# Weight-block sums of six pairs made early and kept in DRAM, and the transposes' PSUM tile cut in two, in a local-attention and feed-forward kernel

## The chip, the cores and the metric

The kernel runs on one NeuronCore of a Trainium2 chip. The metric is the device time of one execution in microseconds. Three runs of the kernel before took 658.18, 658.39 and 658.76 us (median 658.39). Engines are called PE (TensorE matmuls), PEld (TensorE weight loads), DVE (VectorE), ACT (ScalarE), POOL (GpSimd) and SP (SyncE, which only issues DMAs here).

## The reference

Attention over a window of 96 keys and 8 global keys, then a two-layer feed-forward block:

```python
scores = q @ k.T / 8 + bias            # batch 4, heads 8, sequence 768, head_dim 64
a = softmax(scores where global or 0 <= rel < 96)
x = (a @ v)  ->  [3072, 512]
h = x @ w_in                           # [512, 2048]
g = maximum(0.01 * h, h)
out = g @ w_out                        # [2048, 512]
```

All of it is float32. A product of two fp32 matrices is made of three matmuls with operands split into a high and a low part (high*high, high*low, low*high).

## The kernel before

**Work.** The 3072 tokens are 24 steps of 128 tokens, and a step is two units of four heads: 48 units. A unit u runs through loads (Lk, Lv, Lq), scores on PE (S, line 316), bias and row minimum on DVE (B, line 333), exponentials on ACT (E, line 349), sums on DVE (N), the turn of the probabilities, the product with v on PE (V, line 470) and a copy to the feed-forward's input (Xh, lines 480 and 489; Xl). Units 0 to 15 turn the probabilities on PE (T, line 421, against diagonal matrices that POOL makes, G, line 398) into a PSUM tile `ps_tr`, whose two halves are copied to SBUF by two steps, K (half 0, ACT, line 437) and k (half 1; on DVE, line 435, for units 0 to 5, else on ACT). Units from 16 on divide (M, line 386), transpose on DVE (D, line 391) and pass through DRAM (`via`: the store belongs to D, the four fetches are I).

**Feed-forward, chunks 0 to 2.** The steps are cut in chunks of 3, 3, 2, 4, 4, 4, 4. For the first three chunks and each of the 16 column blocks f of w_in there is F (the products with w_in, lines 1030 to 1032), four gate steps g (a ACT line 1042, b DVE line 1044, c ACT line 1046, d DVE line 1048) and H (the products with w_out, lines 1066 to 1068). Meanwhile the weights come in as 32 pieces (Lw) and are turned from float64 words to high and low parts by conversions c (a ACT, b three DVE instructions at lines 801, 803 and 807, c ACT line 811, d DVE line 814).

**Feed-forward, chunks 3 to 6.** Each has 512 tokens and works by pairs p of column blocks, eight pairs to a chunk, 32 in all (Q, y, d, r, h, l, J with the pair's number 0 to 31). The first layer of a pair is a 2x2 block product done with seven block products instead of eight (Q, line 698), which needs four sums of weight blocks. The copy y (ACT, line 729) and line 735 (d, DVE) join the products, line 739 (r) is the leaky maximum, line 742 (h) the high part on ACT, line 745 (l) the low part on DVE, and J (line 753) the product with w_out. Outputs leave by U (lines 759 on DVE, 761 on ACT).

**The sums.** `combine` (lines 652 to 685) makes the four sums of a pair in 16 steps C: 12 on POOL (line 662) and 4 on ACT (line 665, the rounding to a high part). Before the change the sum h1 goes back in place over the w_in block it came from, and the other three go into the place of w_out blocks 4 to 15 in SBUF. So w_out is first stored to DRAM (O, line 706, 16 stores of 512 KB), and only four of its blocks are in SBUF at a time from then on, reloaded through POOL's DMA queue for every pair (R, line 709). The sums are made once, in the first of the four chunks, and stay for the other three.

**Order.** `ORDER` (line 39) is a string of words, one per step, written out beforehand. `step` and `late` issue each word's instructions, and `pin` keeps them in that order on their engine. All engines, and the DMA queues of SP and POOL, take their instructions in this order and none passes another. In the kernel before, the first C stands between F39 and H38, and pair p's sums run beside the products of pair p-2 or p-1 up to pair 6.

Of the kernel before, what the change touches and what calls it, by code (L numbers as in the profile page):

```python
# [67 lines left out]
V20 g34a N22 H33 Xh20 g34b Lv23 M22.0 g34c M22.1 F35 g34d M22.2 M22.3 H34 D22 g35a g35b S23 g35c I22 F36 B23.0 g35d
E23.0 B23.1 H35 B23.2 E23.1 Lk26 B23.3 g36a Lq13 E23.2 g36b V21 E23.3 g36c N23 F37 Lv24 Xh21 g36d M23.0 M23.1 H36
M23.2 g37a M23.3 g37b F38 D23 g37c g37d S24 g38a H37 g38b I23 B24.0 g38c B24.1 E24.0 F39 B24.2 C0.0 E24.1 g38d Lk27  # L70
E24.2 B24.3 C0.1 E24.3 H38 g39a C0.2 N24 g39b C0.4 V22 C0.3 M24.0 g39c M24.1 C0.5 S25 g39d Lv25 Xh22 F40 M24.2 C0.6
Lk28 B25.0 B25.1 Lq14 E25.0 A3.1 B25.2 E25.1 B25.3 H39 g40a M24.3 E25.2 D24 E25.3 C0.8 g40b F41 Y3.4 C0.11 N25 C0.7
I24 g40c M25.0 C0.10 C0.9 V23 M25.1 g40d g41a C0.12 S26 g41b Xh23 Lv26 C0.14 M25.2 H40 C0.13 M25.3 Lk29 g41c B26.0
A3.2 g41d E26.0 F42 B26.1 B26.2 E26.1 A3.3 B26.3 E26.2 D25 H41 E26.3 z3.4 g42a A3.4 Y3.5 F43 Y3.1 g42b I25 N26 C0.15
g42c Y3.6 M26.0 V24 z3.1p g42d g43a S27 M26.1 Lv27 Xh24 g43b H42 Lk30 z3.6p M26.2 g43c M26.3 Lq15 g43d F44 D26 C1.0
# [1068 lines left out]
```

## Time and profile before

| | |
|---|---|
| runs, us | 658.18, 658.39, 658.76 |
| the profiled execution's own time, us | 657.92 |
| its span, us | 656.0 |
| PE busy, us (share of span) | 623.5 (95%) |
| DVE busy, us | 497.8 (76%) |
| ACT busy, us | 280.3 (43%) |
| POOL busy, us | 191.5 (29%) |
| granted TensorE clock over the span | 0.992 of full |
| DMA moved | 118.05 MB, 180 GB/s |

Busy PE means that some matmul was in flight; a gap shorter than a matmul's latency does not show as idle. The span is the recorded program; the own time is what the run's clock says for the same execution, 1.9 us more.

### The profile page before, as it was taken

The page shows a single profiled execution, that of the slowest core. Times are in us where ns is not written, and L with a number is a line of the kernel's source. Part 1 is how long each engine was busy: PE and PEld are TensorE (multiplying, and loading weights), DVE is VectorE, ACT ScalarE, POOL GpSimd, SP SyncE. Part 2 cuts the span into 40 slices and gives each one's busy share as a digit, 9 for nine tenths or more (in the row PEclk, how much of TensorE's full clock was granted, in tenths as well). Part 3 has the DMA queues.
Part 4 walks back from the last instruction along what each step waited for, and adds up shares of the span by engine and source line. Part 5 has one row for each costly group of instructions (what it writes and reads, how often), then busy time and mean ns, then how long its engine had stood idle before and what let it go on. Part 6 is the DMA issues. An engine that isn't in the chain of part 4 may idle for free. (4 is left out here: it accounts for less than half of the span.)

```text
span 656.0 us, 16093 instructions
## 1 busy us (share of the span) xinstructions
PE 623.5 (95%) x6188; PEld 535.1 (82%) x6188; DVE 497.8 (76%) x1277; ACT 280.3 (43%) x801; POOL 191.5 (29%) x265
## 2 busy tenths in 40 slices
PE   5679999999999999989999999999999999999995
PEld 4568888998888877778788888888888888889894
DVE  7899998965766689898997977778977747654542
ACT  4878766546444464523344342334442314211111
POOL 3332410003200067978774200014200015100100
PEclk9799999999999999999999999999999999999999
DMA  8756644497665444527667586775686543433331
GB/s 291 264 197 202 210 160 145 151 409 263 186 195 180 153 152 123 161 92 201 184 196 192 165 279 190 211 213 181 200 269 179 164 121 98 157 101 97 97 97 69
DMA packets 61604, 118.05 MB, mean 180 GB/s; under 512 B 8784, under 2 KB 27216, under 8 KB 61520
## 3 DMA queue, kind: packets, MB, share of 16 engines
q1 hardware_dynamic: 52880, 85.48, 40.6%
q0 software_dynamic: 8640, 31.46, 16.1%
q8 instruction: 51, 0.84, 0.5%
q14 instruction: 33, 0.27, 0.2%
HBM read 90.18 MB, written 26.74 MB: 178 GB/s over the span
## 5 line engine op out<-in xcount | busy, mean ns | idle before, releaser
L742 ACT CAST rounded<-room 128x512 fp32r<-128x512 f32 x64 | 39.7, 620 | 193.5 <-DVE room L739 186.0
L709 POOL DMA_DIRECT2D wo<-w x60 | 32.7, 545 | 229.1 <-PE ps_two L753 221.1
L753 PE MATMUL ps_o<-wo,rounded 128*128 128x512 f32 x320 | 95.1, 394 | 0.5 <-DVE rounded L745 0.5
L753 PE MATMUL ps_two<-wo,rounded 128*128 128x512 f32 x320 | 95.2, 395 | 0.0
L349 ACT ACTIVATE pr<-pr,nmall 128x192 f32<-128x192 f32 (+1 forms) x192 | 83.7, 439 | 14.6 <-DVE nmall L333 14.4
L735 DVE TENSOR_TENSOR room<-ps_o,room 128x256 f32<-128x256 f32 x128 | 53.9, 421 | 34.5 <-PE ps_o L698 26.9
L735 DVE TENSOR_TENSOR room<-ps_q,room 128x256 f32<-128x256 f32 x96 | 40.3, 420 | 32.4 <-PE ps_q L698 30.9
L1030 PE MATMUL ps_h<-rounded,wih 128*128 128x384 f32 (+1 forms) x192 | 62.7, 326 | 1.9 <-ACT atz L1042 1.9
L1031 PE MATMUL ps_h<-rounded,wih 128*128 128x384 f32 (+1 forms) x192 | 61.0, 318 | 0.1
L1032 PE MATMUL ps_h<-rounded,wil 128*128 128x384 f32 (+1 forms) x192 | 61.0, 318 | 0.0
L739 DVE SCALAR_TENSOR_TENSOR room<-room 128x512 f32<-128x512 f32 x64 | 59.4, 927 | 1.9
L753 PEld LDWEIGHTS ps_o<-wo,rounded 128*128 128x128 f32 x320 | 53.7, 188 | 6.7 <-DVE rounded L745 1.0
L753 PEld LDWEIGHTS ps_two<-wo,rounded 128*128 128x128 f32 x320 | 54.0, 188 | 6.1
L698 PEld LDWEIGHTS ps_o<-rounded,wo 128*128 128x128 f32 x384 | 53.9, 188 | 6.2 <-DVE room L735 0.7
L698 PE MATMUL ps_o<-rounded,wo 128*128 128x256 f32 x384 | 56.2, 282 | 0.0
L333 DVE CUSTOM_DVE_ANT_0 pr<-ps_av,nbw 128x192 f32<-128x192 f32 x140 | 42.2, 352 | 13.6 <-ACT room L480 8.1
L698 PE MATMUL ps_q<-rounded,wih 128*128 128x256 f32 x256 | 48.3, 282 | 2.9 <-ACT room L729 2.9
L698 PEld LDWEIGHTS ps_q<-rounded,wih 128*128 128x128 f32 x256 | 41.3, 188 | 6.9 <-ACT room L729 3.9
L386 DVE TENSOR_SCALAR pr<-pr,rs 128x192 f32<-128x192 f32 (+1 forms) x128 | 43.6, 383 | 0.7
L1044 DVE SCALAR_TENSOR_TENSOR atz<-atz 128x384 f32<-128x384 f32 (+1 forms) x48 | 27.2, 567 | 20.7 <-ACT atz L1042 20.6
L1030 PEld LDWEIGHTS ps_h<-rounded,wih 128*128 128x128 f32 x192 | 36.1, 188 | 6.7 <-ACT atz L1042 2.7
L470 PEld LDWEIGHTS ps_av<-room,vr 64*64 64x64 f32 x1472 | 30.5, 134 | 13.2 <-PE ps_two L753 7.1
(134 smaller groups left out, 1433.8 us busy)
## 6 DMA issues: line engine op xcount, KB each, us to landing
wo<-w POOLq DMA_DIRECT2D x60, 512.0 KB, 4.0
via<-pr SPq DMA_DIRECT2D x28, 384.0 KB, 2.7
room<-via SPq DMA_DIRECT2D x112, 96.0 KB, 3.8
kr<-in_kp_dram SPq DMA_DIRECT2D x40, 256.0 KB, 4.0
vr<-in_vp_dram SPq DMA_DIRECT2D x40, 256.0 KB, 3.8
room<-in_wo_dram SPq DMA_DIRECT2D x16, 512.0 KB, 4.4
room<-in_wi_dram SPq DMA_DIRECT2D x16, 512.0 KB, 4.5
w<-wo SPq DMA_DIRECT2D x16, 512.0 KB, 7.6
```

The source lines that it names most:

```text
L333: pin(nc.vector.tensor_tensor_reduce(out=head(u, pr, a, j), in0=own(u, ps[:, j, a * KW:(a + 1) * KW]), in1=nb, scale=-0.125, scalar=3.0e38 ...
L349: pin(nc.scalar.activation(out=p, in_=p, func=AF.Exp, scale=-1.0, bias=nm[:, 2 * a + j:2 * a + j + 1], accum_out=sm[:, 2 * a + j:2 * a + j ...
L386: pin(nc.vector.tensor_scalar(out=p, in0=p, scalar1=rs[:, n:n + 1], scalar2=1.0, op0=ALU.mult, op1=ALU.mult))
L698: tc.keep_in_program_order(nc.tensor.matmul(out, lhsT=lhs[:, k], rhs=rhs[:, k], start=k == 0 and m == 0, stop=k == 1 and m == 2))
L709: pin(nc.gpsimd.dma_start(out=woboth[:, f % 4], in_=w2[f]))
L735: pin(nc.vector.tensor_tensor(out=quarter[i][o], in0=lps[b][:, h * HB:(h + 1) * HB], in1=quarter[a][q], op=ALU.add))
L739: pin(nc.vector.scalar_tensor_tensor(out=t, in0=t, scalar=0.01, in1=t, op0=ALU.mult, op1=ALU.max))
L742: pin(nc.scalar.copy(out=lg(i)[0], in_=lt[i]))
L753: tc.keep_in_program_order(nc.tensor.matmul(o, lhsT=lhs, rhs=rhs, start=f == 0 and m == 0, stop=f == NF - 1 and m == 2))
L1030: tc.keep_in_program_order(nc.tensor.matmul(ps, lhsT=wih[:, k, fs], rhs=xh[:, k, :CT], start=(k == 0), stop=False))
L1031: tc.keep_in_program_order(nc.tensor.matmul(ps, lhsT=wih[:, k, fs], rhs=xl[:, k, :CT], start=False, stop=False))
L1032: tc.keep_in_program_order(nc.tensor.matmul(ps, lhsT=wil[:, k, fs], rhs=xh[:, k, :CT], start=False, stop=(k == NK - 1)))
```

## The change

Pairs 0 to 5 (`NVIA = 6`) get their sums in a work area of SBUF of 8 KB per partition (`early_sums`), not in place. A step b stores the finished area of a pair to a new DRAM tensor `cw` (1 MB, SP's queue). Two steps e load it back through POOL's queue: e.0 brings the three sums h2, h3, h4 (768 KB) to the same region of w_out's place that `combined` reads, e.1 the sum h1 (256 KB) over its w_in block. Pairs 6 and 7 make their sums in place as before. In the new order the first C stands between the last weight conversions, ahead of F19, and the sums of pair 5 end at F41; those of pairs 6 and 7 run beside the products of pairs 0 and 1. The conversions stand up to three pieces earlier (25 pieces end ahead of F17 before, 28 now). w_in's high and low parts become one tile, with a block's halves side by side, so that a sum's operands are 256 elements in a row. And the PSUM tile of two banks that T, the accumulators of chunk 2 and two of J's accumulators use becomes two tiles of one bank each.

```diff
+NVIA = 6
+EARLY_AT = (8, 0, 8, 8, 8, 8)
...
-M23.2 g37a M23.3 g37b F38 D23 g37c g37d S24 g38a H37 g38b I23 B24.0 g38c B24.1 E24.0 F39 B24.2 C0.0 E24.1 g38d Lk27
...
+O2 g17d c31a F18 c30b O3 O4 H17 c31b c30c g18a O5 g18b c31c C0.0 O6 F19 c30d g18c C0.1 g18d O7 c31d C0.2 H18 g19a O8
...
-        ps = ps_x.tile([P, 2, 512], F32, tag="ps_t", name="ps_tr")
+        ps = [ps_x.tile([P, 512], F32, tag=f"ps_t{f}", name="ps_tr") for f in range(2)]
...
-        src = d["ps"][:, :, :6 * HALF].rearrange("p f (j g q) -> p f j g q", j=2, g=3)[:, f, :, g0:]
+        src = d["ps"][f][:, :6 * HALF].rearrange("p (j g q) -> p j g q", j=2, g=3)[:, :, g0:]
...
-                two = ps_x.tile([P, 2, DM], F32, tag="ps_t", name="ps_two")
-                acc[c] = [two[:, tt] for tt in range(CHUNKS[c])]
+                acc[c] = [ps_x.tile([P, DM], F32, tag=f"ps_t{tt}", name="ps_two") for tt in range(CHUNKS[c])]
...
+    cw = dram.tile([NVIA, P, 4, 2, 2 * P], F32, name="cw", bufs=1)
+
+    def early_sums(p):
+        return at(EARLY_AT[p], [8, 2 * P])
...
-        (h2, l2), (h3, l3), (h4, l4) = (combined(p, m) for m in range(3))
-        t1, t2, t3 = (at(o, [2, P]) for o in (14, 15, 20))
-        eng = nc.gpsimd
+        if p < NVIA:
+            b = [early_sums(p)[:, x].rearrange("p (a b) -> p a b", a=2) for x in range(8)]
+            t2, t1, t3 = b[1::2][:3]
+            (h2, l2), (h3, l3), (h4, l4), (h1, l1) = ([x.bitcast(F32R) for x in b[2 * m:2 * m + 2]] for m in range(4))
+        else:
+            t1, t2, t3 = (at(o, [2, P]) for o in (14, 15, 20))
+            (h2, l2), (h3, l3), (h4, l4) = (combined(p, m) for m in range(3))
+            h1, l1 = h21, l21
...
+        elif what == "b":
+            pin(nc.sync.dma_start(out=cw[n].rearrange("p m x d -> p (m x) d"), in_=early_sums(n)))
+        elif what == "e":
+            if part == ".0":
+                to, m = sums3[:, n].rearrange("p m x a b -> p (m x a b)"), slice(0, 3)
+            else:
+                to, m = wiboth[:, 2 * n + 1, 0].rearrange("p x d -> p (x d)"), slice(3, 4)
+            pin(nc.gpsimd.dma_start(out=to, in_=cw[n, :, m].rearrange("p m x d -> p (m x) d")))
```

Three places of the order follow. Line numbers are those of the kernel before and, in the second fence of each, of the changed kernel (line 662 becomes 675, 709 becomes 722, 435 becomes 438, 759 becomes 780).

The first is POOL from the second reload for pair 4 (`wo<-w` is a reload R) to the first for pair 5; the additions between are sums of pair 6. Before:

```order
L709 DMA wo<-w_152 128x1024
L662 TENSOR_TENSOR room<-wih,wil 128x256
L662 TENSOR_TENSOR room<-room 128x256
L662 TENSOR_TENSOR room<-wih,wil 128x256
L662 TENSOR_TENSOR room<-room 128x256
L662 TENSOR_TENSOR wil<-room,wih 128x2x128
L662 TENSOR_TENSOR room<-room 128x256
L662 TENSOR_TENSOR room<-wih,wil 128x256
L662 TENSOR_TENSOR wo<-room,wo 128x256
L709 DMA wo<-w_152 128x1024
```

and now, from the first reload for pair 2 (the three additions are the last of pair 7's sums) to the second for pair 7:

```order
L722 DMA wo<-w_151 128x1024
L675 TENSOR_TENSOR wo<-room,wo 128x256 x3
L722 DMA wo<-w_151 128x1024 x9
L736 TENSOR_TENSOR room<-room 128x512
L722 DMA wo<-w_151 128x1024 x2
```

Of the sums nothing is left here: after pair 7's last, which now come as early as pair 2's reloads, POOL has reloads alone up to the differences of the next chunk's inputs (line 736, 715 before).

The second is DVE in the front of the program, around step k of an early unit. Before:

```order
L807 SCALAR_TENSOR_TENSOR awz<-room,awz 128x512 [waits DVE_49]
L374 TENSOR_SCALAR rs<-sm 128x4 [waits Activation_49,Pool_49]
L375 RECIPROCAL rs<-rs 128x4 [waits DVE_49]
L435 COPY room<-ps_tr 128x2x3x64 [waits Activation_49]
L333 ISA pr,nmall<-ps_sc,nbw 128x192
```

and now:

```order
L828 SCALAR_TENSOR_TENSOR awz<-room,awz 128x512 [waits DVE_49]
L377 TENSOR_SCALAR rs<-sm 128x4 [waits Activation_49,Pool_49]
L378 RECIPROCAL rs<-rs 128x4 [waits DVE_49]
L438 COPY room<-ps_tr 128x2x3x64 [waits PE_49]
L336 ISA pr,nmall<-ps_sc,nbw 128x192
```

The copy k waits for PE's transposes alone, no longer for ACT's copy K.

The third is DVE at the end of the program, the last two output copies U. Before:

```order
L739 SCALAR_TENSOR_TENSOR room<-room 128x512 [waits DVE_49]
L770 TENSOR_LOAD flag [waits DVE_49]
L745 TENSOR_TENSOR btz<-room,rounded 128x512 [waits PE_49,Activation_49]
L759 COPY room<-ps_o 128x512 [waits PE_49,Pool_49]
L759 COPY room<-ps_two 128x512 [waits Activation_49]
```

and now:

```order
L760 SCALAR_TENSOR_TENSOR room<-room 128x512 [waits DVE_49]
L791 TENSOR_LOAD flag [waits DVE_49]
L766 TENSOR_TENSOR btz<-room,rounded 128x512 [waits PE_49,Activation_49]
L780 COPY room<-ps_o 128x512 [waits PE_49,Pool_49]
L780 COPY room<-ps_two 128x512 [waits PE_49]
```

The last copy, too, waits for PE where it waited for ACT's copy of the other bank.

## Rows read from the trace of the kernel before

**Rows 1.** The page's head and its part 1, PE.

```profile
span 656.0 us, 16093 instructions
...
PE 623.5 (95%) x6188; PEld 535.1 (82%) x6188; DVE 497.8 (76%) x1277; ACT 280.3 (43%) x801; POOL 191.5 (29%) x265
```

**Rows 2.** Busy time by stretch: stretch, length, busy us (x instructions) per engine, clock, DMA.

```profile
10.00:48.00 38.00, 27.58 (x653) 23.13 (x650) 33.98 (x114) 28.32 (x91) 14.27 (x24) 0.91 0.73 256
48.00:130.00 82.00, 82.00 (x910) 70.94 (x909) 74.89 (x179) 56.66 (x148) 17.58 (x30) 1.00 0.55 173
130.00:205.00 75.00, 75.00 (x723) 64.19 (x721) 50.95 (x150) 37.93 (x110) 9.74 (x16) 1.00 0.75 259
205.00:241.00 36.00, 36.00 (x452) 30.43 (x451) 24.57 (x81) 17.83 (x62) 7.85 (x10) 1.00 0.49 154
241.00:263.20 22.20, 20.13 (x143) 16.01 (x142) 21.51 (x46) 11.58 (x38) 16.92 (x19) 1.00 0.41 125
263.20:286.60 23.40, 21.58 (x203) 17.84 (x201) 21.11 (x47) 11.48 (x35) 22.30 (x28) 1.00 0.44 136
286.60:354.10 67.50, 63.33 (x610) 52.97 (x610) 60.47 (x125) 22.40 (x68) 44.17 (x58) 1.00 0.63 181
354.10:414.30 60.20, 60.20 (x590) 52.29 (x586) 47.98 (x135) 23.83 (x70) 14.25 (x16) 1.00 0.69 210
```

**Rows 3.** Waits: who for whom, us in total, times, longest.

```profile
ACT wo L665 <- POOL room L662: 13.5, 10, 2.5
...
PE ps_q L698 <- ACT room L729: 2.9, 4, 1.0
...
DVE room L435 <- ACT room L437: 2.1, 2, 1.2
```

**Rows 4.** Timeline from 27 us, ACT and DVE: start, length, instruction, [idle before].

```profile
27.10 0.48 ACT L437 COPY room<-ps_tr 128x384 f32<-128x384 f32 x1 [0.80 <-PE ps_tr L421]
...
27.61 0.56 DVE L435 COPY room<-ps_tr 128x384 f32<-128x384 f32 x1 [0.92 <-ACT room L437]
```

**Rows 5.** Groups by form, POOL, whole span: busy us, mean ns | idle before.

```profile
L709 POOL DMA_DIRECT2D wo<-w x60 | 32.7, 545 | 229.1 <-PE ps_two L753 221.1 <-PE ps_fl L766 3.7 <-DVE rounded L745 3.7
L662 POOL TENSOR_TENSOR room<-room 128x256 f32<-128x256 f32 x32 | 27.8, 872 | 1.8
...
L662 POOL TENSOR_TENSOR wo<-room,wo 128x256 fp32r<-128x256 f32 x24 | 17.9, 755 | 3.0 <-ACT wo L665 2.9
```

**Rows 6.** Groups by form, DVE, 263.2 to 354.1 us.

```profile
L739 DVE SCALAR_TENSOR_TENSOR room<-room 128x512 f32<-128x512 f32 x14 | 20.1, 1435 | 0.4
L735 DVE TENSOR_TENSOR room<-ps_o,room 128x256 f32<-128x256 f32 x28 | 11.6, 416 | 1.1 <-PE ps_o L698 0.5
L386 DVE TENSOR_SCALAR pr<-pr,rs 128x192 f32<-128x192 f32 x24 | 10.7, 484 | 0.1
...
L745 DVE TENSOR_TENSOR rounded<-room,rounded 128x512 fp32r<-128x512 f32 x7 | 8.7, 1244 | 0.0
```

**Rows 7.** Groups by form, DVE, 378.3 to 402.5 us.

```profile
L735 DVE TENSOR_TENSOR room<-ps_o,room 128x256 f32<-128x256 f32 x8 | 3.4, 425 | 1.8 <-ACT pr L349 1.0 <-PE ps_o L698 0.6
L739 DVE SCALAR_TENSOR_TENSOR room<-room 128x512 f32<-128x512 f32 x4 | 2.8, 692 | 0.1
...
L745 DVE TENSOR_TENSOR rounded<-room,rounded 128x512 fp32r<-128x512 f32 x2 | 1.4, 682 | 0.0
```

**Rows 8.** Groups by form, DVE, 130 to 205 us.

```profile
L386 DVE TENSOR_SCALAR pr<-pr,rs 128x192 f32<-128x192 f32 x24 | 6.3, 317 | 0.2
...
L803 DVE SCALAR_TENSOR_TENSOR awz<-room,awz 128x512 int32<-128x512 int32 x5 | 3.5, 692 | 0.2
```

**Rows 9.** Line 706, the sixteen stores O of 512 KB: issue to landing.

```profile
DMA to landing us min/median/max: 3.8/7.6/7.8
```

**Rows 10.** Timeline from 646 us, ACT and DVE, the last two copies.

```profile
648.73 0.59 ACT L761 COPY room<-ps_two 128x512 f32<-128x512 f32 x1 [1.56 <-PEq L1086]
649.35 0.69 DVE L759 COPY room<-ps_two 128x512 f32<-128x512 f32 x1 [1.31 <-ACT room L761]
```

More of the change, by code (lines that the diff above doesn't have):

```diff
@@ L161, in fast_path @@
 @with_exitstack
[L162 removed]
+def fast_path(ctx, tc, qp, kp, vp, wi, wo, nvec, weights, wiboth, woboth, nmall, out, B, H, S):
     nc = tc.nc
@@ L642, in fast_path @@
     quarter = [[x[:, h * HB:(h + 1) * HB] for h in range(2)] for x in lt]
+    sums3 = woboth.rearrange("p f x d -> p (f x d)")[:, 8 * DM:].rearrange("p (q m x a b) -> p q m x a b", q=NF // 2, m=3, x=2,
+                                                                   a=2)
     def combined(p, n):
-        i, half = divmod(3 * p + n, 2)
-        return [w[:, 4 + i, half * 2 * P:(half + 1) * 2 * P].rearrange("p (a b) -> p a b", a=2) for w in (woh, wol)]
+        return [sums3[:, p, n, x] for x in range(2)]
+    cw = dram.tile([NVIA, P, 4, 2, 2 * P], F32, name="cw", bufs=1)
+    def early_sums(p):
+        return at(EARLY_AT[p], [8, 2 * P])
     def first_weights(p, row, col):
-        fs = slice((2 * p + row) * P, (2 * p + row + 1) * P)
-        return [w[:, 2 * col:2 * col + 2, fs] for w in (wih, wil)]
+        return [w[:, 2 * p + row, col].rearrange("p (a b) -> p a b", a=2) for w in (wih, wil)]
     def combine(p, n):
@@ L1025, in products @@
     wih, wil = weights[:2]
[L1026 to L1027 removed]
+    NK = wih.shape[2] * wih.shape[3] // P
     ps = psum.tile([P, CT], F32, tag="ps_h", name="ps_h")
     for k in range(NK):
[L1030 to L1032 removed]
+        wh, wl = (w[:, f, k // 2, k % 2 * P:(k % 2 + 1) * P] for w in (wih, wil))
+        tc.keep_in_program_order(nc.tensor.matmul(ps, lhsT=wh, rhs=xh[:, k, :CT], start=(k == 0), stop=False))
+        tc.keep_in_program_order(nc.tensor.matmul(ps, lhsT=wh, rhs=xl[:, k, :CT], start=False, stop=False))
+        tc.keep_in_program_order(nc.tensor.matmul(ps, lhsT=wl, rhs=xh[:, k, :CT], start=False, stop=(k == NK - 1)))
     return ps
@@ L1079, in tile_kernel @@
         n = NK * NF * P
-        wih = keep.tile([P, n], F32R, name="wih").rearrange("p (a b) -> p a b", a=NK)
-        wil = keep.tile([P, n + 16], F32R, name="wil")[:, :n].rearrange("p (a b) -> p a b", a=NK)
+        wiboth = keep.tile([P, 2 * n + 16], F32R, name="wi")[:, :2 * n].rearrange("p (f c x d) -> p f c x d", f=NF, c=2, x=2)
+        wih, wil = (wiboth[:, :, :, x] for x in range(2))
         woboth = keep.tile([P, 2 * n + 16], F32R, name="wo")[:, :2 * n].rearrange("p (f x d) -> p f x d", f=NF, x=2)
```

248 lines of the change are left out of this document (122 added, 126 removed).

## Prediction

> **What bounds the kernel now.** I read the page's head first: PE is busy for 623.5 of 656.0 us [rows 1], so at most some 30 us of matmul idle exist, and the question is only where they lie and which of them the change touches. The table by stretches answers that [rows 2]. The reader is to see three kinds of rows in it. From 10 to 48 us PE is idle for 10.4 us (38.00 less 27.58) while DVE is busy for 33.98 of 38: the front is DVE's. From 48 to 241 us PE has no idle at all, in three rows running, and DVE's share falls from 91% (74.89 of 82) to 68% (24.57 of 36). From 241 to 354.1 us PE is idle again, 2.07, 1.82 and 4.17 us, and just there POOL is fullest (16.92, 22.30, 44.17 us) and DVE nearly so (21.51 of 22.2, 21.11 of 23.4, 60.47 of 67.5). From 354.1 us on the idle is gone. The last three rows are cut at the starts of pairs 0, 2, 7 and 12: pairs 2 to 6 took 67.5 us, 13.5 each, and the next five, with the same products, 60.2 us, 12.0 each.
>
> Why DVE is full beside the sums is seen in its groups. In 263.2 to 354.1 us the leaky maximum of line 739 takes 1435 ns, line 745 (into `rounded`) 1244 and the division of line 386 484 [rows 6]. Where POOL has only reloads, lines 739 and 745 take 692 and 682 [rows 7], and line 386 takes 317 where POOL is mostly idle [rows 8]. Line 735, with one input in PSUM, takes 416 and 425, no difference [rows 6, 7]. So DVE lost 14 x 0.743 + 24 x 0.167 + 7 x 0.562 = 10.4 + 4.0 + 3.9 = 18.3 us beside some 70 of the 96 POOL instructions of the sums: 0.26 us for each. POOL itself needs 0.755 to 0.872 us for one [rows 5]. In-order ACT pays too: its rounding steps waited 13.5 us for POOL, ten times, up to 2.5 [rows 3], with the next copies queued behind.
>
> **The change, part by part.** The sum is made against the profiled execution's own 657.92 us, 0.47 below the median; the 1.9 us of it that lie around the span are taken as they are.
>
> *Front, copies K and k.* The copies of the early units go from one after the other to side by side. The timeline shows ACT's copy at 27.10 for 0.48 us and DVE's at 27.61, DVE having been idle 0.92 us for it [rows 4]; DVE waited so twice, 2.1 us [rows 3]. The wait for PE's transposes stays, ACT's 0.48 goes: twice 0.5, **-1.0** on the engine that sets this stretch. Ends: 0 (another wait follows) and -2.1 (both waits go whole).
>
> *Conversions up to three pieces earlier.* A piece is four DVE instructions of about 0.69 us at most (row of line 803 [rows 8]), so 2.8; three are 8.4 us more for DVE by 130 us, where it has 82 - 74.89 = 7.1 us idle [rows 2]. What doesn't fit is **+1.3**. Ends: 0 (part of it falls behind 130 us) and +4.9 (half the idle is bound to waits: 8.4 - 3.5).
>
> *Sums of six pairs moved to about 130 to 241 us.* 72 POOL instructions come there, 54 to 63 us [rows 5], and 24 roundings on ACT. POOL has 111 - 17.6 = 93 us free [rows 2]. DVE would lose 72 x 0.26 = 18.7 us and has 24.1 + 11.4 = 35.5 idle, less loaded by the conversions that left. PE has no idle in these rows and the gate steps have room between F and H, so the cover holds; but steps get longer, and some of them end later than their H. I take **+0.7**. Ends: 0, as in the row of 205 to 241, and +10.3, if PE idled here as from 241 to 263.2 (2.07 of 22.2, 9.3%, of 111 us). The 205 row is nearer: DVE's load here would be about 77%, not 97%.
>
> The page "SBUF — State Buffer" of the Trainium skill, section "Who interferes with whom", says that a VectorE instruction with two SBUF inputs contends with a GpSimd one that reads SBUF, and that the second to issue waits until the first has finished. By that rule alone every moved sum could hold DVE for its whole 0.8 us, 58 us against 35.5 idle, some 22 us too many, where the sum above has 0.7; the trace agrees on which instructions suffer (739 and 745, not 735), and its price is 0.26.
>
> *241 to 263.2 us.* The sums of pairs 0 and 1 go; the input differences and four more loads come (12 loads in all, 0.545 us of POOL each [rows 5], with POOL now free). Of the 2.07 us idle I take **-1.2**. Ends -2.1 and +2: the differences write over the area of the last store. A store of 512 KB took 7.6 us to land [rows 9], so one of 1 MB may take 15.2, and the differences, with the input roundings on ACT behind them, would start late. The earlier stores hold up only the next pair's sums.
>
> *Pairs 0 and 1.* Pairs 6 and 7 are summed here in place of 2 and 3, so POOL stays as full. Besides, the order puts three more divisions and one more rounding rest on DVE: 3 x 0.484 + 1.244 = 2.7 us [rows 6] where 2.3 are idle [rows 2]. **+1.0**; ends 0 and +2.7.
>
> *Pairs 2 to 6.* POOL's order has reloads only, as in pairs 7 to 11, and DVE has the same instructions in both. 67.5 goes to 60.2 [rows 2], less 0.8 us because the second five hold one unit with fewer keys and pair 2 inherits what pair 1 left late: **-6.5**. Ends -7.3 and -3.3 (half, if part of the idle is DVE's order).
>
> *Tail.* The last copy stood ready with ACT's but started when that ended, 649.35 against 648.73 [rows 10]; the end of the span hangs on it. **-0.6**; ends -0.3 (its DMA issues behind the other's) and -0.7. PE's work, the copies' lengths and the loads of w_out are the same: nothing. The operands of the sums being in one row instead of two is nothing either, 0.872 and 0.755 us already mixing both.
>
> Sum: -1.0 + 1.3 + 0.7 - 1.2 + 1.0 - 6.5 - 0.6 = -6.3, so 651.6 for such an execution and **652.1 us** for the median.
>
> **The rivals.**
>
> *DVE becomes the bound in the front* (48 to 137 us). For it: 91% busy now, and up to 8.4 us more. Against: the three pieces are ahead only late, one or two by the time F11 runs. Price: the upper end, +4.9 for +1.3: 655.7 us.
>
> *POOL's sums stop the gates* (130 to 241 us): slower. Every moved sum may hold up DVE, and behind a rounding that waits on ACT stand the gates' copies, on which the next F and H wait. It decides when DVE loses more than 35.5/72 = 0.49 us per sum, twice the 0.26 seen, or when PE's idle share gets to the 9.3% of 241 to 263.2 us. Price: +10.3 for +0.7, 661.7 us. For it: that very stretch, with the same kind of gate steps. Against: there DVE was 97% busy, and ACT waited for POOL only 13.5 us in all.
>
> *The sums were not what held the pairs.* PE's largest wait of its own among the products is for ACT's copy of line 729 (2.9 us, four times [rows 3]), not for a sum, and other causes may keep it. Then -6.5 falls away: 658.6 us. Against: pairs 7 to 11 have those steps without the idle.
>
> **How the numbers follow.** A measurement of this kernel can tell 0.2% (1.3 us) from no change. The forecast gets 0.63 (649.0 to 655.4 for its own terms: 0.8 lower if pairs 2 to 6 give their whole 7.3, 2.0 if conversions and moved sums cost nothing; on the other side two terms at half their upper ends), DVE in front 0.14, POOL's sums 0.11, sums without effect 0.07, and 0.05 for lower or mixed cases. Faster: 0.63 + 0.13 + 0.04 = 0.80. Within 0.2%: 0.07 + 0.01 = 0.08. Slower: 0.11 + 0.01 = 0.12. The range 649.0 to 658.0 takes in the forecast, the DVE rival and the mixed cases; the slower rival, most of the third, and some 0.03 below are left out, together 0.2.
>
> **What would show it.** The pairs' starts: about 12.2 us apart from pair 2 on; 12 to 13 for pairs 0 and 1. Line 739 near 0.69 us in pairs 2 to 6, and lines 1044 and 1048 longer than before from 135 to 240 us. PE without idle from 48 to 241 us; idle there, or F47 later than before, speaks for the first two rivals: with DVE above 95% before 130 us for the first, with ACT waiting for POOL's sums after 135 us for the second. Pairs 2 to 6 at 13.5 us would be the third. The two copies at the end should start within 0.1 us of each other. A time above 658 us makes the prediction wrong.

## The result and the profile after

The changed kernel took 662.69 us (median of 20 runs, 656.79 to 667.41) against 658.17 for the kernel before on the same chip (655.94 to 659.06): a ratio of 1.0057, 95% interval 1.0042 to 1.0073. It is slower by 0.6%, where 652.1 us was forecast. Ratios here and below leave out runs more than 1.5% above the same kernel's fastest. The profiled execution took 663.38 us, its span 661.6.

The page's head and part 1 of the changed kernel answer to [rows 1]:

```profile
span 661.6 us, 16121 instructions
...
PE 622.5 (94%) x6188; PEld 534.9 (81%) x6188; DVE 490.9 (74%) x1277; ACT 279.9 (42%) x801; POOL 197.7 (30%) x277
```

PE and DVE have a little less to do than before and the span is 5.6 us longer: time went into waiting. The table by stretches (columns as in [rows 2]) shows where:

```profile
10.00:48.00 38.00, 27.74 (x710) 22.81 (x707) 36.19 (x121) 30.53 (x101) 15.76 (x24) 1.00 0.81 276
48.00:130.00 82.00, 81.83 (x907) 70.43 (x906) 79.33 (x180) 58.02 (x144) 19.75 (x32) 1.00 0.61 197
130.00:205.00 75.00, 73.05 (x668) 62.02 (x666) 52.22 (x139) 39.63 (x120) 42.64 (x58) 1.00 0.74 255
205.00:241.00 36.00, 32.78 (x381) 27.14 (x380) 23.58 (x64) 15.57 (x53) 19.69 (x27) 1.00 0.70 224
241.00:263.20 22.20, 18.99 (x163) 15.63 (x161) 18.49 (x45) 10.46 (x33) 16.32 (x20) 1.00 0.98 326
263.20:286.60 23.40, 17.77 (x188) 15.16 (x192) 14.45 (x41) 9.79 (x31) 8.35 (x11) 0.85 0.69 202
286.60:354.10 67.50, 66.54 (x610) 57.59 (x603) 52.40 (x143) 20.59 (x66) 15.26 (x22) 1.00 0.63 190
```

PE had no idle from 130 to 241 us before [rows 2]; now it has 1.95 and 3.22 us there, then 3.21 and 5.63, the last with the clock down to 0.85. The last column but one is new in kind: from 241 to 263.2 us the DMA engines are busy for 0.98 of the time and move 326 GB/s, where it was 0.41 and 125. What was to be gained was gained (286.6 to 354.1 us is nearly free of idle) and lost before.

Who waited, from 185 to 275 us:

```profile
POOL room L675 <- DMA cw<-room: 27.5, 3, 11.8
...
ACT room L678 <- POOL room L675: 7.5, 5, 4.6
...
PE ps_av L473 <- DMA room<-via: 6.2, 4, 4.7
```

The first row is the sums of pairs 3 to 5 (line 675), which stood still until the store b of the pair before had landed, since they use its work area; the second is ACT's roundings behind them. The last is V, waiting for its fetches I. Two transfers show the pattern. SP's queue at 181 us issues b2 (line 726) and, 0.47 us later, the store D (line 363):

```profile
180.79 0.38 SPq L726 DMA_DIRECT2D cw<-room  x1
181.26 0.39 SPq L363 DMA_DIRECT2D via<-pr  x1
181.70 1.20 SPq L287 DMA_DIRECT2D qs<-in_qp_dram  x1
188.50 1.91 SPq L369 DMA_DIRECT2D room<-via  x4
```

The fetches (line 369) wait for D to land, 7.2 us later. Before, the seven stores D from 175 to 230 us took 2.3 to 2.9 us. The second is the chain that ended last, from 247 us (start, length, what):

```profile
247.56 6.59 DMA via<-pr
...
258.22 9.11 DMA room<-via
267.47 0.70 PE ps_av L473 x5
...
270.38 0.43 PE ps_two L1088
...
273.95 0.23 PE ps_two L1088
```

A store of 6.6 us and a fetch of 9.1 hold V, and PE stands for 1.06 and 4.75 us. After that an H matmul takes 0.43 us until 272 us and 0.23 from 273 on: the granted clock was at half (1.2 for 2.4 GHz) from 265.2 to 272.0 us.

What filled the DMA engines is on POOL's queue (start, length, instruction, [idle before]; line 732 is a load e, `wo` 768 KB and `wi` 256 KB, line 736 a difference):

```profile
241.25 1.10 POOL L732 DMA_DIRECT2D wo<-cw  x2
242.34 1.07 POOL L732 DMA_DIRECT2D wi<-cw  x2
244.69 0.56 POOL L732 DMA_DIRECT2D wo<-cw  x1 [1.28 <-PE ps_two L1089]
247.92 5.78 POOL L736 TENSOR_TENSOR room<-room 128x512 f32<-128x512 f32 x4 [2.67 <-DMA cw<-room]
253.67 3.13 POOL L742 TENSOR_TENSOR rounded<-room,rounded 128x512 fp32r<-128x512 f32 x2
256.75 1.10 POOL L732 DMA_DIRECT2D wo<-cw  x2
257.84 0.54 POOL L732 DMA_DIRECT2D wi<-cw  x1
260.12 0.53 POOL L732 DMA_DIRECT2D wo<-cw  x1 [1.75 <-PE ps_two L1089]
```

Nine of the twelve loads, 5.25 MB, go out within 19 us: five as soon as pair 5's last sum (ahead of the first row) lets POOL's queue on, with b5 (1 MB) at 241.3 us among them, and four behind the differences. The eight fetches that V waits for, of 64 KB each, fall among these four: the five issued from 254.2 to 256.4 us took 2.5 to 4.0 us, the three issued from 257.3 to 258.2 us, behind the loads of 256.75 us, 4.9 to 9.1.

### The profile page after: what moved, and what is told of

Its sections match the earlier page's. It is cut to its first block, busy times and chain, and to the rows that moved or that the text cites. A ratio compares the mean times of both kernels' runs of the same rounds, so it can differ in the third digit from the quotient of the medians.

```text
span 661.6 us, 16121 instructions
## 1 busy us (share of the span) xinstructions
PE 622.5 (94%) x6188; PEld 534.9 (81%) x6188; DVE 490.9 (74%) x1277; ACT 279.9 (42%) x801; POOL 197.7 (30%) x277
## 4 chain that ended last, share of the span: by engine, by line
PE 72%; DMA 10%; DVE 8%; ACT 4%; issue 2%; SPq 2%; POOL 1%; DVEq 0%; ACTq 0%; POOLq 0%
PE ps_q L711 13%; PE ps_two L774 12%; PE ps_o L774 12%; PE ps_o L711 9%; DMA room<-via 4%; PE ps_av L473 4%; DMA via<-pr 3%; PE ps_av L319 3%; PE ps_h L1051 3%; PE ps_h L1053 3%; PE ps_h L1052 3%; PE ps_o L1087 3%; PE ps_o L1089 3%; PE ps_o L1088 2%; ACT pr L352 2%
## 5 line engine op out<-in xcount | busy, mean ns | idle before, releaser
L1051 PE MATMUL ps_h<-rounded,wi 128*128 128x384 f32 (+1 forms) x192 | 62.6, 326 | 1.2 <-ACT atz L1063 1.1
L1052 PE MATMUL ps_h<-rounded,wi 128*128 128x384 f32 (+1 forms) x192 | 61.0, 318 | 0.6 <-POOL rounded L497 0.6
L1053 PE MATMUL ps_h<-rounded,wi 128*128 128x384 f32 (+1 forms) x192 | 60.9, 317 | 0.0
L711 PE MATMUL ps_q<-rounded,wi 128*128 128x256 f32 x384 | 55.3, 280 | 0.4 <-ACT room L750 0.4
L711 PEld LDWEIGHTS ps_q<-rounded,wi 128*128 128x128 f32 x384 | 51.8, 189 | 3.8 <-ACT room L750 0.7
L760 DVE SCALAR_TENSOR_TENSOR room<-room 128x512 f32<-128x512 f32 x64 | 48.1, 753 | 1.7
L675 POOL TENSOR_TENSOR room<-room 128x256 f32<-128x256 f32 (+1 forms) x56 | 45.4, 821 | 8.2 <-ACT room L678 5.8
L473 PE MATMUL ps_av<-room,vr 64*64 64x64 f32 (+1 forms) x1472 | 37.8, 239 | 8.1 <-DMA room<-via 6.7
```

The costliest lines, as they stand in the source:

```text
L473: tc.keep_in_program_order(nc.tensor.matmul(av[out, a, cols], lhsT=v[rows, t, j, :], rhs=near(rows, j, t, f), start=n == 0, stop=n + 1 == ...
L675: pin(nc.gpsimd.tensor_tensor(out=out, in0=a, in1=b, op=op))
L711: tc.keep_in_program_order(nc.tensor.matmul(out, lhsT=lhs[:, k], rhs=rhs[:, k], start=k == 0 and m == 0, stop=k == 1 and m == 2))
L760: pin(nc.vector.scalar_tensor_tensor(out=t, in0=t, scalar=0.01, in1=t, op0=ALU.mult, op1=ALU.max))
L1051: tc.keep_in_program_order(nc.tensor.matmul(ps, lhsT=wh, rhs=xh[:, k, :CT], start=(k == 0), stop=False))
L1052: tc.keep_in_program_order(nc.tensor.matmul(ps, lhsT=wh, rhs=xl[:, k, :CT], start=False, stop=False))
```

## The experiments

The table sums up the fourteen runs. "F25" to "end" say by how many us the first matmul of that step (Q0: of pair 0), or the end of the span, comes later than in the kernel before, in the profiled executions. Runs of one group shared a chip and the runs of the kernel before.

| group | kernel | median us | ratio to before (95%) | F25 | H44 | Q0 | Q7 | end |
|---|---|---|---|---|---|---|---|---|
|  | changed | 662.69 | 1.0057 (1.0042 to 1.0073) | -2.2 | +3.2 | +11.7 | +5.3 | +5.6 |
| 1 | e1_psum | 656.81 | 0.9980 (0.9967 to 0.9994) | -2.0 | -2.0 | -2.0 | -1.6 | -1.7 |
| 1 | e2_small | 650.90 | 0.9875 (0.9850 to 0.9901) | +0.7 | -1.1 | -0.6 | -7.1 | -6.0 |
| 1 | e3_nowait | 662.08 | 1.0067 (1.0044 to 1.0090) | -1.3 | -3.2 | +7.5 | +1.1 | +2.0 |
| 1 | e4_spread | 661.95 | 1.0068 (1.0043 to 1.0092) | -1.7 | +9.8 | +10.0 | +4.0 | +4.1 |
| 2 | e5_both | 654.81 | 0.9936 (0.9902 to 0.9969) | -1.3 | -2.3 | +3.0 | -3.0 | +3.2 |
| 2 | e6_poolq | 657.29 | 0.9985 (0.9960 to 1.0011) | -1.0 | +3.8 | +4.0 | -2.0 | -1.1 |
| 2 | e7_five | 654.46 | 0.9951 (0.9927 to 0.9975) | -0.4 | -1.7 | -1.3 | -5.1 | -3.9 |
| 3 | e10_five_only | 656.63 | 0.9992 (0.9967 to 1.0018) | +1.0 | +0.7 | +1.1 | -2.5 | -2.8 |
| 3 | e9_five_moved | 652.07 | 0.9920 (0.9898 to 0.9942) | -0.5 | -2.7 | -2.3 | -6.2 | -5.7 |
| 3 | e8_split | 655.90 | 0.9977 (0.9957 to 0.9998) | -1.3 | +1.3 | +1.6 | -4.4 | -3.2 |
| 4 | e11_best | 653.16 | 0.9932 (0.9905 to 0.9958) | -0.7 | -2.7 | -2.4 | -6.2 | -5.3 |
| 4 | e12_no_sixth | 661.46 | 1.0056 (1.0035 to 1.0078) | -1.8 | +0.8 | +8.1 | +1.7 | +2.3 |
| 5 | e13_no_burst | 657.32 | 0.9999 (0.9974 to 1.0024) | -0.9 | +5.2 | +5.5 | -0.7 | -0.4 |
| 5 | e14_thin | 651.07 | 0.9901 (0.9875 to 0.9927) | -0.6 | -2.3 | -2.0 | -7.0 | -6.4 |

**e1_psum.** The kernel before with the five edits to the PSUM tile alone (the diff above shows three of them).

> The kernel before with the PSUM tile of the transposes cut in two, and nothing else of the change. In the profile of the change PE stood 2.65 us earlier than before at F0 and the end after the last pair came 1.0 us sooner. If both come from the PSUM tile alone: 2.6 + 1.0 = 3.6 us less than before, some 654.5 us, ratio 0.9945. If the front's gain is only the 1.0 us of the prediction and the rest was an accident of the granted clock: 1.6 less, ratio 0.9976. If the gain came from the earlier conversions or the new layout of w_in: 0.6 to 1.0 less, ratio 0.999.

Measured: 1.3 us less. PE stands 1.96 us earlier from F3 to pair 4, 1.57 from pair 7 on, and the end gains 0.1 more. So the PSUM tile gives about what its two terms said together (1.6), not the 2.8 us that PE stood ahead at F3 in the changed kernel. Part of both figures may go with the clock from 10 to 48 us, 0.91 before and 1.00 in both of these; what parts the two isn't shown.

**e2_small.**

```diff
-pin(nc.sync.dma_start(out=cw[n].rearrange("p m x d -> p (m x) d"), in_=early_sums(n)))
+pin(nc.sync.dma_start(out=cw[n, :, 0, 0], in_=early_sums(n)[:, 0]))
...
-to, m = sums3[:, n].rearrange("p m x a b -> p (m x a b)"), slice(0, 3)
+to = sums3[:, n, 0, 0].rearrange("p a b -> p (a b)")
```

(and e.1 likewise.)

> The changed kernel, each store b and each load e cut to 128 KB (b 1/8 of its bytes, e.0 1/6, e.1 1/2), at the same places of the order; it leaves out storing and reloading the rest of the sums, and POOL's sums hardly wait for the stores any more. Theory 1, the bytes of b and e stand before the store D and the fetches I of the attention and delay V and the gates: D's store at 181 us back from 7.2 to about 2.5 us, fetches at 258 us from 9.1 to under 4, PE's idle of 11.6 us from 185 to 275 falls under 3, the stretch at half clock behind it goes; 12 to 13 us less than the changed kernel, some 650 us. Theory 2, the wait of the next pair's sums for the store's landing: goes here too, so the same 650; the next run tells these apart. Theory 3, the moved order of D, I and V among the gates: nothing changes, 661 to 663 us.

Measured: 11.8 us less than the changed kernel, PE's idle from 185 to 275 us 2.1 us for 12.3 (90 less the busy time; 2.9 before). The whole loss goes with the transfers. It also shows the sums alone. The stretch from 150 to 241 us, of the kernel before and of e2_small:

```profile
150.00:241.00 91.00, 91.00 (x1031) 76.87 (x1030) 61.78 (x206) 46.39 (x154) 17.59 (x26) 1.00 0.58 184
```

```profile
150.00:241.00 91.00, 90.60 (x979) 76.41 (x978) 70.58 (x200) 50.15 (x168) 57.23 (x79) 1.00 0.57 174
```

With 39.6 us more of POOL, DVE is busy for 8.8 us more, which it had idle, and PE idles 0.4. The 8.8 understates the price, for four conversion instructions and three divisions have left the stretch. The divisions that stand in both (line 386, 389 in e2_small) show it best:

```profile
L386 DVE TENSOR_SCALAR pr<-pr,rs 128x192 f32<-128x192 f32 x32 | 8.4, 316 | 0.2
```

```profile
L389 DVE TENSOR_SCALAR pr<-pr,rs 128x192 f32<-128x192 f32 x32 | 15.7, 541 | 0.1
```

All DVE instructions that stand in both took 11.9 us longer beside 47 more sums: 0.25 us for each, the prediction's 0.26.

**e3_nowait and e4_spread.** The first stores from elsewhere, the second moves loads in the order (some of the places are left out):

```diff
-in_=early_sums(n)))
+in_=wiboth[:, 12:14].rearrange("p f c x d -> p (f c x d)").bitcast(F32)))
```

```diff
-M25.0 e2.0 g41c
+M25.0 g41c
...
-E26.3 e3.0 g45a e4.0 N26 g45b e5.1 F46 e5.0 M26.0
+E26.3 g45a N26 g45b F46 M26.0
...
-Q0.6 E27.2
+Q0.6 e2.0 E27.2
...
-Q1.5 B29.1
+Q1.5 e3.0 B29.1
```

> The changed kernel, where b stores the same 1 MB from two blocks of w_in instead of from the work area, so no sum and no difference waits for it, and the bytes that move are the same; the stored values are not the sums. Theory 1 (bytes): the waits of line 675 for b (27.5 us) go, the gap of 2.25 us at 235 us goes, but D's store and the fetches stay at 7 and 9 us: 2 to 4 us less than the changed kernel, 659 us. Theory 2 (the waits for the area): 9 to 13 us less, 650 to 653 us. Theory 3: no change.

> The changed kernel with the eight loads e of pairs 2 to 5 moved in the order from 225 to 260 us into pair p-1, one pair each; b as it is. Theory 1: between 241 and 263 us 4 MB fewer are moved, DMA share from 0.98 to about 0.6, the fetches at 258 us under 5 us, the gaps of 1.06 and 4.75 us at 262 and 267 us and the half clock behind them go (about 9 us), the losses up to 245 us (4 to 5 us) stay: 653 to 655 us. Against it: 1 MB more per pair in pairs 0 to 4 may come late there, up to 3 us. Theory 2 and 3: no change, 661 to 663 us.

Measured: 662.1 and 662.0, neither gains. Theory 1 had said it of neither, theory 2 of e4_spread alone, and theory 3 fell with e2_small: none has both. In e3_nowait the sums wait no more (H44 at -3.2), and then PE stands 8.4 us for V's fetches; from 241 us on:

```profile
241.00:263.20 22.20, 13.97 (x133) 11.78 (x132) 16.82 (x28) 7.61 (x22) 13.75 (x15) 0.93 1.03 346
```

In e4_spread the DMA share there is 0.62, V doesn't wait, and another wait stands in its place. POOL's queue, and ACT behind it:

```profile
242.00 1.10 POOL L732 DMA_DIRECT2D wo<-cw  x2
254.58 4.29 POOL L736 TENSOR_TENSOR room<-room 128x512 f32<-128x512 f32 x3 [11.48 <-DMA cw<-room]
...
255.87 0.62 ACT L739 CAST rounded<-room 128x512 fp32r<-128x512 f32 x1 [6.72 <-POOL room L736]
```

The difference (line 736) writes where b5's area was. b5, issued at 242.8 us right behind two loads of 768 KB, took 11.6 us. Two waits stood one over the other, and each alone is enough.

**e5_both, e6_poolq, e7_five.** Both edits; then two tries to keep the sums, with the loads as in e4_spread: b on POOL's queue behind the pair's last sum (and e.0 of pairs 0 and 1 among pair 5's), and five early pairs, where pair 5's sums take the places of pair 6's, pair 6's those of pair 7's, and pair 7's stand in pairs 2 and 3.

```diff
-pin(nc.sync.dma_start(out=cw[n].rearrange("p m x d -> p (m x) d"), in_=early_sums(n)))
+pin(nc.gpsimd.dma_start(out=cw[n].rearrange("p m x d -> p (m x) d"), in_=early_sums(n)))
...
-C2.15 E18.3
+C2.15 b2 E18.3
```

```diff
-NVIA = 6
-EARLY_AT = (8, 0, 8, 8, 8, 8)
+NVIA = 5
+EARLY_AT = (8, 0, 8, 8, 8)
...
-C5.15 B25.1 F41 B25.2 E25.1 e0.0 b5 B25.3
+B25.1 F41 B25.2 E25.1 e0.0 B25.3
...
-Q0.1 z3.2 C6.0 g47c
+Q0.1 z3.2 C5.0 g47c
```

> The edits of e3_nowait and e4_spread together: b stores its 1 MB from two blocks of w_in (nothing waits for it, the stored values are not the sums), and the loads e of pairs 2 to 5 come one pair each in pairs 0 to 3. Theory 1, now: three waits stand one behind another between 192 and 272 us (the sums and then the input differences for the landing of b; the attention's fetches behind the loads e), and taking one away lets the next one decide, which is why either edit alone gained nothing. Then both together give most of it back: PE idle between 190 and 275 us under 4 us, Q0 at most 2 us later than before, 652 to 655 us, ratio 0.991 to 0.996. Rival: the stores D of the attention behind b (7.2 us for 2.4) are what costs, and b moves the same bytes here: 658 us or more, with idle of 3 us or more between 190 and 245 us. Rival: the loads e in pairs 0 to 3 cost there what they cost at 241 to 263 us: Q0 early, but pairs 0 to 4 some 5 us longer than in the changed kernel, 657 us.

> The changed kernel made to keep the early sums without these waits, computing everything: the store b goes out on POOL's queue right behind the last sum of its pair (5 to 6 us earlier than on SP's queue, and not ahead of a store D there), e.0 of pairs 0 and 1 stand among pair 5's sums, those of pairs 2 to 5 one pair each in pairs 0 to 3. Theory 1: the sums of pairs 3 to 5 wait under 3 us each for b, D's store back under 4 us, the differences wait under 4 us for b5; 652 to 655 us, ratio 0.991 to 0.996. If the two queues' transfers hinder one another as those of one queue do, D and I stay at 6 to 9 us beside b: 657 to 660 us.

> The changed kernel with the early sums for five pairs alone (pair 5 is summed in place as 6 and 7 are, in pairs 0 to 2), so that no store stands just ahead of the input differences, and the loads e of pairs 2 to 4 one pair each in pairs 0 to 2; b stays on SP's queue. Theory 1: the wait of the differences (11.5 us in e4_spread) goes and with it the gap of 4.0 us and what lies behind it; the losses up to 235 us (some 3 to 4 us) stay; pair 2 costs about 1.3 us more than in the changed kernel: 655 to 657 us. If the differences were not what cost in e4_spread: 661 us or more.

Measured: 654.8, 657.3 and 654.5. Both edits together give back 7 to 8 us where each alone gave nothing (the profiled execution of e5_both was one of its longest, with a wait of V and a stretch at half clock at pair 9; Q0 and Q7 lie ahead of these). The second rival there falls: Q0 to Q7 take 84.9 us as in the changed kernel (84.5) with the loads among them. e6_poolq shows that another queue doesn't part the transfers: with b3 issued by POOL at 196.0 us, two fetches that SP issued at 196.6 and 198.7 took 6.6 and 4.8 us, one at 221.6, behind b4 and two loads, 8.7, and the difference still waited 7.1 us for b5. The Trainium skill says so in "DMA: Bandwidth & Descriptors", section "Issuing engines are not separate DMA queues": transfers of all issuing engines run on the same 16 DMA engines and interleave. The trace agrees.

**e10_five_only, e9_five_moved, e8_split.** e7_five with its loads back in place; e7_five with three stores moved; six pairs with b in four parts (fences: e9_five_moved and, without its order, e8_split).

```diff
-D17 C2.15 E18.3
+D17 C2.15 b2 E18.3
...
-S19 b2 g27a
+S19 g27a
...
-H30 b3 M21.0 g31a M21.1 M21.2 M21.3 D21 F32
+H30 M21.0 g31a M21.1 M21.2 M21.3 D21 b3 F32
...
-C4.12 I22 P31.1
+C4.12 I22 b4 P31.1
```

```diff
-pin(nc.sync.dma_start(out=cw[n].rearrange("p m x d -> p (m x) d"), in_=early_sums(n)))
+m = int(part[1:])
+pin(nc.sync.dma_start(out=cw[n, :, m], in_=early_sums(n)[:, 2 * m:2 * m + 2]))
```

> e7_five with the loads e of pairs 2 to 4 back where the changed kernel has them, so that only one of its two edits is left: no store stands ahead of the input differences any more, but ten of the twelve loads e still come between 218 and 260 us. Theory 1 (each of the two waits is ready to take the other's place): V waits for its fetches behind the loads again, 3 us or more of idle at 255 to 270 us, 658 to 661 us. If the wait of the differences alone was the whole loss: 654 to 656 us, as e7_five.

> e7_five with three stores b at other places of SP's queue: b2 ahead of the fetches I that it followed, so 5 us earlier and not just ahead of the store D18; b3 behind the store D21 instead of ahead of it; b4 behind the fetches I22, 3 us earlier. Bytes and sums are the same. If the stores D behind a b are what costs the 2.8 us at F33 to F35: D18 and D21 land in 2.5 to 4 us (now 5.5), F35 within 1.5 us of the kernel before, and 0.5 to 2 us less than e7_five, as far as the later order does not give that back anyway (e7_five is level with before again at F43): 652.5 to 654.5 us. If they cost nothing in the end: 654 to 655.

> All six early pairs kept and everything computed: b cut in four stores of 256 KB in SP's queue, at the places of e9_five_moved (for pair 5 the h1 part goes ahead during its sums, the one that the first difference waits for first among the rest), e.0 of pairs 0 and 1 among pair 5's sums, the loads of pairs 2 to 5 one pair each in pairs 0 to 3. Theory 1: the differences wait for 256 KB instead of 1 MB, some 3 us instead of 11.5, the sums of pairs 3 to 5 under 5 us each, Q0 at most 1.5 us later than before, pairs 2 to 6 at 61 us: 651 to 654 us. If the landing of b5 is no sooner for being cut: 656 to 659 us.

Measured: 656.6, 652.1 and 655.9. e10_five_only is the surprise: ten loads stand where the changed kernel has them and nothing waits for them. PE has no idle from 241 to 272 us at a DMA share of 0.81. Theory 1 as put there (the loads' bytes are enough) is wrong. It is 2.2 us above e7_five by the medians; in the profiled executions 1.3 us lie between the two at F25 already, ahead of any load. In e9_five_moved the stores D behind b2 and b3 landed in 3.9 and 2.5 us, where e7_five's took 5.5 and 5.9; b4 stood ahead of pair 4's last two sums, so the two low parts they make were not stored; e11_best mends that. In e8_split the difference still waits 7.5 us for b5.

**e11_best and e12_no_sixth.** e9_five_moved with b4 behind C4.15; the changed kernel without b5, e5.0 and e5.1.

> As e9_five_moved, with b4 behind the last sum of pair 4 (there it stood two sums too early, so pair 4's last low parts were not stored): everything is computed. Nothing but b4's place differs, 0.5 us later on SP's queue: 651.5 to 654 us, ratio 0.990 to 0.994, at least as fast as e7_five. If the stores behind the fetches gained nothing and e9's time came from b4 leaving early: 654 to 655 us, as e7_five.

> The changed kernel without b5, e5.0 and e5.1: the sums of pair 5 are still made early, but neither stored nor reloaded (its products take what stands there). The ten other loads, all sums, roundings and the order stay. Theory 1, as the last runs leave it: what costs the 8 us at 241 to 272 us is the sixth pair's store with its loads, which come on top of the ten others in front of the differences and the fetches: DMA share there from 0.98 to about 0.85, no idle for the fetches at 262 to 268 us, no half clock behind it, some 7 to 9 us less than the changed kernel: 654 to 656 us. If instead the sums of pair 5 on POOL and their roundings on ACT are what e10_five_only saved: 660 us or more.

Measured: 653.2, below the kernel before with its whole interval, though not told apart from e7_five (0.9951, 0.9927 to 0.9975), and 661.5, against the expectation. The sixth pair's bytes are not it either. What differs between e10_five_only and e12_no_sixth is when the same loads leave. POOL's queue of e10_five_only:

```profile
234.54 0.53 POOL L732 DMA_DIRECT2D wo<-cw  x1 [5.11 <-PE ps_two L1089]
237.32 0.53 POOL L732 DMA_DIRECT2D wo<-cw  x1 [2.25 <-PE ps_two L1089]
237.84 0.54 POOL L732 DMA_DIRECT2D wi<-cw  x1
242.31 0.53 POOL L732 DMA_DIRECT2D wi<-cw  x1 [3.92 <-PE ps_h L1053]
244.52 0.54 POOL L732 DMA_DIRECT2D wo<-cw  x1 [1.68 <-PE ps_two L1089]
```

and of e12_no_sixth:

```profile
240.13 1.10 POOL L732 DMA_DIRECT2D wo<-cw  x2
241.21 0.55 POOL L732 DMA_DIRECT2D wi<-cw  x1
242.34 0.53 POOL L732 DMA_DIRECT2D wi<-cw  x1 [0.58 <-PE ps_h L1053]
244.56 0.54 POOL L732 DMA_DIRECT2D wo<-cw  x1 [1.68 <-PE ps_two L1089]
```

In the first each load leaves when PE frees its place (the releaser in brackets); in the second they stand behind pair 5's last sum until 240 us, and five of them, 2.75 MB, leave within 5 us, ahead of D at 247.5, which takes 6.15 us (4.66 in e10_five_only). So its fetches go out 1.5 us later, and that decides where they fall against the next two loads, of 768 KB each. These leave at the same time in both kernels, e10_five_only and then e12_no_sixth:

```profile
255.33 1.10 POOL L732 DMA_DIRECT2D wo<-cw  x2
```

```profile
255.37 1.10 POOL L732 DMA_DIRECT2D wo<-cw  x2
```

In e10_five_only the eight fetches went out from 252.1 to 255.3 us, ahead of these loads. In e12_no_sixth they went out from 253.7 to 256.9 us: the first four took 2.0 us, the last four, behind the first load or both, 3.6 to 7.3. Landing of the eight, shortest, median, longest, in the two:

```profile
DMA to landing us min/median/max: 1.9/2.2/2.7
```

```profile
DMA to landing us min/median/max: 2.0/2.8/7.3
```

**e13_no_burst and e14_thin.** Three of those loads among the sums; and e11_best with eight sums to a pair.

```diff
-C5.6 B24.3
+C5.6 e0.0 B24.3
...
-C5.10 F40 C5.9 M24.0 g39c M24.1 C5.11 g39d
+C5.10 e1.0 F40 C5.9 M24.0 g39c M24.1 C5.11 e3.1 g39d
...
-E25.1 e0.0 B25.3 E25.2 D24 e1.0 E25.3 H40 e3.1 g41a
+E25.1 B25.3 E25.2 D24 E25.3 H40 g41a
```

```diff
-g47d C5.1 Lk29 y0.1 E27.3 d0a H47 Y3.3 C5.2 N27
+g47d Lk29 y0.1 E27.3 d0a H47 Y3.3 C5.1 N27
...
-Lv29 C6.0 S29
+Lv29 C5.7 S29
...
-Q2.2 C7.0 d2a
+Q2.2 C6.0 d2a
...
-Q4.2 B31.3
+Q4.2 C7.0 B31.3
```

> e12_no_sixth with three of its ten loads at another place of POOL's queue and nothing else: e.0 of pairs 0 and 1 and e.1 of pair 3 stand among pair 5's sums, where their places are free, instead of behind the last of them. In e12_no_sixth the sums hold them back and six loads (2.75 MB) leave at 240.1 to 244.6 us, just ahead of two units' stores D; in e10_five_only the same six left at 234.5 to 244.5. If this burst is what delays the attention's round trip: D's store at 247 us back from 6.2 to under 4 us, the fetches from 7.0 to under 5, the gaps of 2.2 and 2.3 us at 261 and 264 us and the half clock behind them go; 653 to 656 us (e12_no_sixth: 661.5). If it is pair 5's sums, by DVE, ACT or POOL's time: 660 us or more.

> e11_best with the 48 sums of pairs 5, 6 and 7 spread over pairs 0 to 5, eight to a pair, instead of sixteen to a pair in pairs 0 to 2. DVE has 12 us of idle in the five pairs without sums (60.2 less 48.1), 2.4 to a pair; eight sums at 0.26 us cost 2.1, sixteen 4.2. If the price of a sum is DVE's idle, it is hidden now: Q0 to Q7 from 87.1 to about 84.5 us, 650.5 to 652 us, ratio 0.987 to 0.990. If a sum costs the same wherever it stands (by the roundings in ACT's order, or the reloads they stand among): no change, 653 us; if they now hold up the reloads R in POOL's queue: slower.

(The expectation counts six loads; it is five, with the bytes as given.) Measured: 657.3, so 4.1 us less than e12_no_sixth by three words of the order (3.7 by the ratios, for the chips differ). The two gaps at 261 and 264 us are gone, and from H44 to Q0 nothing more is lost (+5.2 to +5.5; e12_no_sixth +0.8 to +8.1). The fetches issued from 250 to 262 us:

```profile
DMA to landing us min/median/max: 1.8/2.0/3.2
```

The median is above the 653 to 656 expected because this execution lost more ahead of H44: b4 took 8.2 us to land, pair 5's sums, the roundings and the gates stood behind it, and PE has gaps of 2.2 and 2.3 us at 237 and 245 in that chain. From 241 us on the loss takes two things together: the burst, which makes D late, and the loads behind the differences, which the late fetches then fall behind. In e13_no_burst D took 4.7 us, and all but the last fetch went out ahead of these loads (259.8 us). e4_spread has a late D (6.5 us) and no such loads, and its eight fetches took 1.9 to 2.3 us; e10_five_only has the loads and no late D; V waits in neither. The margin is small, for e10_five_only's last fetch left with the first load; whether its runs, 652.9 to 661.2 us, fall on both sides of it isn't shown.

e14_thin took 651.07 us, the fastest kernel of this study that computes everything: 1.0% below the kernel before, and below the changed kernel. Q0 to Q7 take 85.9 us, where e11_best took 87.1 and 84.5 was expected. That thinning the sums is worth its 2 us isn't settled, for the two intervals overlap (0.9901, 0.9875 to 0.9927, and 0.9932, 0.9905 to 0.9958).

## Why the prediction was wrong

Its terms against the changed kernel's profile, by the starts of PE's steps:

| term | forecast | ends | measured |
|---|---|---|---|
| front, copies K and k (to F3) | -1.0 | 0, -2.1 | -2.8 (-2.8 to +0.4 over the fifteen profiles) |
| conversions (F3 to F25) | +1.3 | 0, +4.9 | +0.5 |
| moved sums (F25 to H44) | +0.7 | 0, +10.3 | +5.4 |
| 241 to 263.2 us (H44 to Q0) | -1.2 | -2.1, +2 | +8.6 |
| pairs 0 and 1 | +1.0 | 0, +2.7 | +0.1 |
| pairs 2 to 6 | -6.5 | -7.3, -3.3 | -6.5 |
| pairs 7 to 31 | 0 | | +1.2 |
| tail | -0.6 | -0.3, -0.7 | -0.9 |
| sum | -6.3 | | +5.6 |

The step that failed is "241 to 263.2 us": "the input differences and four more loads come (12 loads in all, 0.545 us of POOL each)". A load was priced by what it costs the engine that issues it, and not by the 6 MB that the twelve bring, nor by who else uses the DMA engines then and is issued behind them. The table of before [rows 2] had the number to ask with: a DMA share of 0.41 and 125 GB/s in that stretch, 2.8 MB in 22.2 us, onto which 5.25 MB of loads and a store of 1 MB came. The attention's round trip through DRAM, which stands on V's path, was in none of the terms. The upper end, +2, was reasoned from b5's landing alone, a wait that is there (2.67 us in the changed kernel, 11.5 in e4_spread), but the dearer one is the fetches'. Of the 8.6 us, 5.8 are V's two gaps and some 2.3 the 4.5 us that PE then worked at half clock.

The term of the moved sums was mis-sized, and for a reason not named. "The earlier stores hold up only the next pair's sums": they also stood ahead of the stores D, and the sums they held up held ACT's roundings and the gates. The forecast for DVE held: "DVE's load here would be about 77%" was 70.58 of 91, 78%, in e2_small, with PE idle for 0.4 us, and the 0.26 us for a sum came out as 0.25.

Smaller terms. In the front the mechanism came: k's waits of 2.1 us for ACT are gone (0.2 us for PE is left). Its size can't be read from one execution. In the three profiles with the split tile that spent 6.8 us at half clock there, as the kernel before's did (e6_poolq, e9_five_moved, e11_best), F3 comes 1.0 to 1.5 us earlier, near the -1.0. At the tail the size came by another way than forecast: the two copies start 0.65 us apart, not within 0.1, but each follows its own bank's last product, DVE's within 0.04 us where it was 0.71. Pairs 7 to 31 had no term: every kernel with the early sums loses 0.8 us or more from Q7 to Q12, e1_psum nothing, and why stays open. And the range's lower end is mis-summed, for 652.1 - 0.8 - 2.0 is 649.3.

The Trainium skill's rule in "SBUF — State Buffer", section "Who interferes with whom", which the prediction weighed, gave 58 us of DVE and 22 too many by a hold-up of the whole 0.8 us for every sum. Measured are 11.9 us for 47 sums, 0.25 each; the trace agrees on the contention, and not every sum held an instruction up for its whole length.

The rivals. "POOL's sums stop the gates" came nearest in time (661.7), in its place, in its sign (ACT waited 7.5 us for the sums) and in what it does to the gates, but not by its mechanism: DVE's loss per sum stayed at half of its 0.49 us, and the sums were late for a store. "DVE becomes the bound in the front" didn't come (0.5 us), though DVE was busy for 79.33 of the 82 us from 48 to 130, above the 95% named as its sign. "The sums were not what held the pairs" is refuted, -6.5 to the digit. No rival had the DMA engines.

The gain itself was right: with the transfers out of the way (e2_small) the change is worth 7.2 us (658.07 to 650.90), where the terms summed to 6.3. What is shown of that is the -6.5 of pairs 2 to 6 (-6.6 in e2_small); that the sum comes near is in part luck, for in its profile F25 to H44 gains 1.8 us (+0.7 forecast) and H44 to Q0 loses 0.5 (-1.2 forecast).

## What to carry to other kernels

Price a transfer twice: by its issue, and by its bytes in the stretch where it will run, beside the small transfers on the critical path that share the DMA engines; a share that goes from 0.4 to 1.0 is a reason to look, though the share alone doesn't settle it (e4_spread lost 11.5 us at 0.62, e10_five_only nothing at 0.81). Ask of every small transfer which large one is issued just ahead of it, on any queue: here fetches of 64 KB took 2.0 us ahead of two loads of 768 KB and up to 7.3 behind them. Loads held back behind late work come out in one burst, and moving three of them forward among that work was worth 4 us. When removing one wait gains nothing, look for a second one under it before giving up the theory.

## What the runs showed that was not expected

A store of 384 KB took 7.2 us behind one of 1 MB, for 2.3 to 2.9 us in the kernel before, and a fetch of 64 KB behind three loads 9.1 us.

PE's granted clock fell to half at the waits: for 6.8 us in the changed kernel, from 265.2 us on, within the second of the two gaps (261.3 to 262.3 and 262.7 to 267.5); in e10_five_only, without these gaps, it stays at 1.00 from 241 to 272 us. With the 2.3 us lost at half clock the gaps cost about 1.4 times their own length. In the front the clock differs between kernels whose instructions there are the same (1.00 in the changed kernel from 10 to 48 us, 0.82 in e2_small), and F3 stands 2.9 us apart in these two. Whether that is why the changed kernel's runs spread over 10 us isn't shown.
